# Threshold attention and an ELU feed-forward on one core: another order of the first 45 attention steps, and score rows placed 64 numbers further along the PSUM banks

## The chip, the cores and the metric

The kernel runs on one core of a Trainium2 chip, as one program with one launch. Its engines work side by side, each through its own queue in order: TensorE (PE in the profile, its weight loads PEld), VectorE (DVE), ScalarE (ACT), GpSimd (POOL), and SyncE (SP), which issues nearly all transfers. The metric is the device time of one execution in microseconds (us). Times are given as the median of several executions, and the profile belongs to one execution of its own.

## The reference: what is computed

Eight sequences with eight heads of 576 positions and 64 numbers go through attention in which every score further than `tau` below the maximum of its row is dropped. The result, with the heads side by side, goes through a feed-forward of 512 to 2048 to 512 numbers with ELU between. All is float32; the two weight matrices come as float64, so the kernel has to convert them on the chip.

```python
scores = (q @ k.T) / 8                       # 8 x 8 x 576 x 576
keep   = scores >= max(scores, axis=-1) - tau
attn   = where(keep, exp(scores - max), 0)
attn   = attn / (sum(attn, axis=-1) + 1e-9)
x      = attn @ v                            # -> (8*576, 512)
h      = x @ w_in                            # 512 -> 2048
g      = where(h > 0, h, exp(min(h, 0)) - 1)
out    = g @ w_out                           # 2048 -> 512
```

## The kernel before

**Units of work.** Two heads of a sequence form a pair; there are 32 pairs, four to a sequence. Pair number `pr` has 64 rows of q for one head below 64 for the other, so that the two heads use the two halves of TensorE's rows at once. The queries of a pair are cut into five blocks: blocks 0 to 3 have 128 queries of each head, and block 4 (`NC`) has the remaining 64 queries of both heads as one block of 128 rows. A *step* is one block of one pair: `scores` on TensorE into PSUM, maximum (`max_of`), `exp_of` on ScalarE, `bound_of` on GpSimd, `mask_of` on VectorE (it also sums), sum and reciprocal (`reciprocal_of`), and `normalize` on GpSimd.

The normalized rows are then turned so that keys stand on partitions. There are two ways. `turn_parts` turns them on TensorE, in nine transposes (six for block 4) with an identity matrix, from which ScalarE copies them into the tile `wTa` (blocks 0 and 1, "part 0") or `wTb` (blocks 2 to 4, "part 1"). `turn_squares` transposes squares of 32 by 32 on VectorE, writes the result to DRAM (`there`, four transfers of 144 KB) and `fetch` reads it back in its new order (576 KB). `values` multiplies with v once all blocks of a part are there, and `values_out` copies the result into `xt`, the input of the feed-forward.

**Three stretches.** The first 45 steps (pairs 0 to 8) are written by `early_tasks`. Every operation there is a `task` with a nominal time, a key and the tasks it needs; the value of the key in the table `MOVED` is added to the time, and all tasks are issued in the order of these times, what they need first. So `MOVED` and the nominal times set only the order in which each engine's queue holds its work. A key names the operation, the kind of the step (a letter) and its block. The remaining 23 pairs are written by `tail_step` and `wide_step`, whose scores, two blocks at a time, stand in one PSUM tile of five banks (`wide_scores`); the list `agenda` places the other work there, again with `MOVED`. After the last pair, a stretch of feed-forward alone ends the kernel.

**The first 45 steps in detail.** The order is pair after pair, blocks 0 to 4. The 20 steps of the first sequence have no feed-forward to do, because `xt` of the first sequence is complete only with pair 3. In them `turn_part` puts extra transposes of the identity in front of the real ones (`spare`: 14 in a step, 20 in the earliest, none where the next step's block is 2 or 4); `idle` puts 28 and 16 more at the start. Nothing reads their results. From step 20 on the feed-forward of the first sequence's 512 main rows is done in plain form: `ffn1` (8 units for each of two chunks of 256 rows) and `ffn2_plain` (8 units for each chunk). Each unit is two *halves*, and `SHARES` (steps 20 to 34) and `QUOTA` (steps 35 to 44) say how many halves a step may issue: 14 and 15 in five steps. A half is left for later when the weights it needs are not converted yet (`needs`, `progress`).

The weights come in 32 pieces of 512 KB (`load_w`), and each takes two passes of ScalarE, two of VectorE and one of GpSimd. Seven pieces are handled in steps 4 to 19, then two in a step. Each of the four staging tiles `wst` is loaded again when the piece before in it is finished (`convert_end`), and all these loads go through SP's queue together with those of q, k and v and the squares' transfers.

At step 35 (`SWITCH`) the staging memory is given up for other tiles (`leave_early`). From there all steps turn by squares (`SQUARES`; of the steps before, only step 33 does). In steps 35 to 42 `make_in` forms sums of blocks of w_in on VectorE (three additions each, eight times) and writes them to DRAM, 384 KB each, and in steps 40 to 44 `change_in` changes w_in in place on GpSimd; the later stretches do the feed-forward with seven products instead of eight by them (`first_product`, `second_round`).

Of the kernel before, what the change touches and what calls it, by code (L numbers as in the profile page):

```python
# [18 lines left out]
MOVED = {  # L19
    "adda10": 2.75, "adda40": -0.7, "addb10": -0.45, "addb11": -0.96, "addb20": 0.4, "addb21": 0.54, "addb30": 0.08,  # L20
    "addb31": 0.42, "addb40": -0.13, "addb41": -0.45, "addz40": 1.52, "chd0": -1.67, "chd1": 0.66, "chd3": 5.2,
    "cka3": 1.4, "ckb3": -3.64, "ckc3": -0.46, "ckd3": -1.83, "ckz3": -1.37, "cqa2": 6.78, "cqb2": -3.01,
    "cqc2": -0.22, "cqd2": 2.27, "enda10": 2.38, "enda40": -0.2, "endb00": -0.03, "endb01": 1.48, "endb10": -0.28,
    "endb20": -1.25, "endb21": -1.07, "endb30": 1.25, "endb31": -0.02, "endb40": -0.99, "endb41": 0.29,
    "endz40": 1.58, "exp0a0": 0.24, "exp0a1": -1.03, "exp0a2": 0.05, "exp0a3": 1.07, "exp0a4": -0.35, "exp0b1": -0.97,
    "exp0b2": -0.37, "exp0b3": 1.51, "exp0b4": 0.45, "exp0c0": 0.41, "exp0c1": 3.53, "exp0c2": 0.65, "exp0c4": -0.53,
    "exp0d0": 0.12, "exp0d1": -2.91, "exp0d4": -0.42, "exp0z0": -1.78, "exp0z1": -0.69, "exp0z2": -1.71,
    "exp0z3": 1.1, "exp0z4": -1.32, "exp1a0": 0.27, "exp1a2": -1.45, "exp1b0": -0.12, "exp1b1": -0.6, "exp1b2": 0.26,
    "exp1b3": -0.56, "exp1c0": -1.22, "exp1c1": 1.42, "exp1c3": -0.54, "exp1d1": 0.28, "exp1d3": 0.23, "exp1z0": 4.71,
    "exp1z2": 0.39, "exp1z3": 2.23, "f0.0": -2.08, "f1.0": -0.13, "f1.1": 0.2, "f10.0": 0.05, "f11.0": -0.04,  # L30
    "f12.1": 0.12, "f13.1": -0.5, "f14.0": 0.02, "f15.1": -0.06, "f16.0": 0.04, "f16.1": 0.69, "f16.2": -0.14,
    "f17.0": -0.28, "f18.1": 0.12, "f2.0": -5.54, "f2.1": -0.25, "f2.2": 0.7, "f20.1": -1.03, "f21.0": 0.13,
    "f22.1": -0.19, "f23.0": 0.08, "f23.1": 2.72, "f23.2": 0.07, "f25.0": 0.39, "f26.0": -0.08, "f26.1": 0.42,
    "f3.0": 0.35, "f5.0": -0.32, "f5.1": 4.32, "f6.1": -0.54, "f7.0": -0.01, "f9.0": 0.35, "f9.1": 1.94,
    "fbound0": -0.14, "fbound1": 0.93, "fbound4": -0.36, "fe00": 0.1, "fe10": 0.37, "fe11": 0.3, "fe20": -0.6,
    "fetchc0": 0.68, "fetchc1": 1.8, "fetchc3": 1.11, "fetchc4": 2.68, "fetchd0": -1.89, "fetchd1": -3,
    "fetchd2": 0.42, "fexp00": 0.1, "fexp20": 0.25, "fexp31": 0.12, "ffetch0": 1.19, "ffetch1": -0.24,
    "ffetch2": -0.52, "ffetch3": -0.65, "fkcopy": -0.11, "floadk": -2.59, "floadq": 2.51, "fm00": -3.15,
    "fm01": -0.49, "fm11": -2.07, "fm20": 1.6, "fm21": -0.43, "fmask00": 1.48, "fmask01": -0.63, "fmask10": 0.68,
    "fmask11": 0.02, "fmask30": -0.16, "fmask31": 0.36, "fmask4": 0.2, "fmax00": -0.03, "fmax01": -0.65,  # L40
    "fmax10": 0.91, "fmax11": 0.5, "fmax20": -0.99, "fmax21": -0.15, "fmax30": 0.04, "fmax31": -0.17, "fmax4": 0.36,
# [96 lines left out]
def kernel(  # L138
# [45 lines left out]
    psum = {"t": banks.enter_context(tc.tile_pool(name="ps_t", bufs=2, space=PSUM))}  # L184

    first = ExitStack()
    psum["s"] = first.enter_context(tc.tile_pool(name="ps_s0", bufs=3, space=PSUM))

    ident = wstage.tile([P, P], FP32, name="ident", bufs=1)
    make_identity(nc, ident)  # L190

    tau_sb = const.tile([P, 1], FP32, name="tau_sb")
# [1454 lines left out]
```

## Time and profile before

| | before |
|---|---|
| median of 3 executions | 1311.3 us (1310.9 to 1311.52) |
| the profiled execution | 1310.99 us |
| its span, first to last instruction | 1309.2 us |
| PE busy | 1294.1 us (99%), 6971 instructions |
| PEld busy | 1007.7 us (77%) |
| DVE busy | 1016.5 us (78%) |
| POOL busy | 802.8 us (61%) |
| ACT busy | 559.6 us (43%) |
| DMA | 248.94 MB, mean 190 GB/s |
| first score of steps 10, 20, 35 | 51.57, 96.59, 206.03 us |
| first score of the first `tail_step` | 287.34 us |

Times inside the profile count from the span's start. A group of instructions is named by line, engine and operation, then what it writes and reads by the program's names, its shape, how many there were, busy time and mean duration, and at the end the idle time of the engine before them with what ended it. A float32 matmul is two instructions on TensorE. A table of stretches gives the busy time of each engine in each stretch with its number of instructions in parentheses, the granted TensorE clock (1.00 is full), the mean busy share of the 16 DMA engines and what they moved. A timeline row is start, duration, engine, line, operation, names, form and count of merged neighbours; a matmul's duration includes its way through the array, so its cost in a row of matmuls is read from the distance of the starts.

### The profile page before, as it was taken

The page shows a single profiled execution, that of the slowest core. Times are in us where ns is not written, and L with a number is a line of the kernel's source. Part 1 is how long each engine was busy: PE and PEld are TensorE (multiplying, and loading weights), DVE is VectorE, ACT ScalarE, POOL GpSimd, SP SyncE. Part 2 cuts the span into 40 slices and gives each one's busy share as a digit, 9 for nine tenths or more (in the row PEclk, how much of TensorE's full clock was granted, in tenths as well). Part 3 has the DMA queues.
Part 4 walks back from the last instruction along what each step waited for, and adds up shares of the span by engine and source line. Part 5 has one row for each costly group of instructions (what it writes and reads, how often), then busy time and mean ns, then how long its engine had stood idle before and what let it go on. Part 6 is the DMA issues. An engine that isn't in the chain of part 4 may idle for free.

```text
span 1309.2 us, 21968 instructions
## 1 busy us (share of the span) xinstructions
PE 1294.1 (99%) x6971; PEld 1007.7 (77%) x6971; DVE 1016.5 (78%) x2199; ACT 559.6 (43%) x1216; POOL 802.8 (61%) x1186
## 2 busy tenths in 40 slices
PE   9999999999999999999999999999999999999998
PEld 7667656556788887777777787777777888888887
DVE  6878886879888988898889979897989882545534
ACT  5677763225252535344444434352525260421320
POOL 4667875777466765766576747574858473624533
PEclk9999999999999999999999999999999999999999
DMA  6344655987888988898979888989899875221211
GB/s 138 77 106 125 177 111 140 258 229 219 222 233 237 258 227 251 220 268 209 245 211 264 231 234 225 258 235 240 229 253 256 221 215 173 92 73 60 93 61 33
DMA packets 323379, 248.94 MB, mean 190 GB/s; under 512 B 208832, under 2 KB 285120, under 8 KB 323264
## 3 DMA queue, kind: packets, MB, share of 16 engines
q1 hardware_dynamic: 321328, 247.06, 69.2%
q8 instruction: 55, 0.90, 0.3%
q10 hardware_dynamic: 1936, 0.48, 0.2%
q14 instruction: 60, 0.49, 0.1%
HBM read 162.40 MB, written 85.07 MB: 189 GB/s over the span
## 4 chain that ended last, share of the span: by engine, by line
PE 92%; DVE 4%; DMA 1%; issue 1%; POOL 1%; SPq 1%; ACT 0%; DVEq 0%; POOLq 0%; ACTq 0%
PE f L1378 29%; PE f L1238 29%; PE sc L625 8%; PE sc L685 7%; PE f L776 4%; PE rt L438 3%; PE sc L367 3%; PE f L736 3%; PE pv L578 2%; PE sc L677 1%; PE sc L672 1%; PE pv L573 1%; DVE w L428 1%; DMA there<-x 0%; POOL w L401 0%
## 5 line engine op out<-in xcount | busy, mean ns | idle before, releaser
L401 POOL TENSOR_SCALAR w<-w,rs 128x576 f32<-128x576 f32 x196 | 164.8, 848 | 80.7 <-DVE rs L435 65.5
L632 DVE TENSOR_REDUCE mx<-sc 128x1 f32<-128x576 f32 x207 | 148.2, 749 | 35.7 <-PE sc L625 33.0
L642 ACT ACTIVATE w<-sc,mx 128x576 f32<-128x576 f32 x115 | 83.0, 740 | 114.4 <-DVE mx L632 96.8
L1238 PE MATMUL f<-xt,sw 128*128 128x256 f32 x512 | 123.8, 384 | 0.8 <-ACT xt L695 0.5
L1238 PE MATMUL f<-xt,w_in_sb 128*128 128x256 f32 x512 | 122.4, 381 | 0.3 <-ACT w L1252 0.3
L638 POOL TENSOR_SCALAR th<-mx,ntau 128x2 f32<-128x2 f32 (+1 forms) x115 | 34.3, 298 | 141.2 <-DVE mx L632 141.2
L512 DVE STREAM_TRANSPOSE x<-w 128x512 f32<-128x512 f32 (+2 forms) x146 | 98.1, 706 | 13.5 <-POOL w L401 12.9
L1238 PEld LDWEIGHTS f<-xt,w_in_sb 128*128 128x128 f32 x512 | 96.1, 190 | 16.1 <-ACT w L1252 3.3
L1238 PEld LDWEIGHTS f<-xt,sw 128*128 128x128 f32 x512 | 93.7, 190 | 18.2 <-ACT xt L695 0.9
L625 PE MATMUL sc<-kT,qT 64*128 64x512 f32 (+4 forms) x736 | 107.5, 423 | 0.0
L1238 PE MATMUL f<-x,w_in_sb 128*128 128x256 f32 x448 | 106.1, 379 | 1.3 <-ACT g L1299 1.3
L625 PEld LDWEIGHTS sc<-kT,qT 64*128 64x128 f32 x736 | 80.8, 186 | 34.2 <-issue 16.8
L1378 PE MATMUL f<-w_out_sb,g 128*128 128x256 f32 x448 | 107.1, 382 | 0.0
L1378 PE MATMUL f<-w_out_sb,s 128*128 128x256 f32 x448 | 107.0, 382 | 0.0
L1378 PE MATMUL f<-t,s 128*128 128x256 f32 x448 | 105.8, 379 | 0.0
L1325 POOL TENSOR_TENSOR s<-g 128x256 f32<-128x256 f32 x104 | 80.3, 778 | 29.4 <-PE f L1378 20.1
L646 DVE SCALAR_TENSOR_TENSOR w<-sc,th,w 128x576 f32<-128x576 f32 x115 | 89.7, 810 | 10.3 <-ACT w L642 10.1
L1238 PEld LDWEIGHTS f<-x,w_in_sb 128*128 128x128 f32 x448 | 85.0, 190 | 13.3 <-ACT g L1299 1.7
L1378 PEld LDWEIGHTS f<-w_out_sb,g 128*128 128x128 f32 x448 | 84.1, 190 | 12.9 <-issue 0.7
L1378 PEld LDWEIGHTS f<-t,s 128*128 128x128 f32 x448 | 85.1, 190 | 11.6
L1378 PEld LDWEIGHTS f<-w_out_sb,s 128*128 128x128 f32 x448 | 84.2, 190 | 12.3
L401 POOL TENSOR_SCALAR e<-e,rs 128x576 f32<-128x576 f32 x92 | 68.5, 748 | 35.8 <-DVE rs L435 34.5
(189 smaller groups left out, 2853.7 us busy)
## 6 DMA issues: line engine op xcount, KB each, us to landing
there<-x SPq DMA_DIRECT2D x412, 144.0 KB, 3.5
wTb<-there SPq DMA_DIRECT2D x53, 576.0 KB, 6.3
wTa<-there SPq DMA_DIRECT2D x50, 576.0 KB, 5.0
sw<-win_sums SPq DMA_DIRECT2D x62, 384.0 KB, 4.3
t<-wout_sums SPq DMA_DIRECT2D x45, 512.0 KB, 5.4
qm<-in_q_dram SPq DMA_DIRECT2D x124, 72.0 KB, 4.5
vm<-in_v_dram SPq DMA_DIRECT2D x64, 128.0 KB, 3.4
wst<-in_moe_w_in_dram SPq DMA_DIRECT2D x16, 512.0 KB, 4.0
```

The costliest lines, as they stand in the source:

```text
L367: nc.tensor.matmul(scs[h][:, a, :HALF], qs[r], kT[r, k0 : k0 + HALF], start=True, stop=True)
L401: nc.gpsimd.tensor_scalar(wv, wv, st["rs"][:, h : h + 1], 1.0, ALU.mult, ALU.mult)
L512: nc.vector.transpose(x[:, :, c0 : c0 + nc_], src.rearrange("p (c g n) -> p g c n", c=nc_, n=T))
L625: on_banks(nc.tensor.matmul(o, qT[r, i * P : (i + 1) * P], kT[r, k0 : k0 + n], start=True, stop=True, skip_group_check=True), o)
L632: on_banks(nc.vector.tensor_reduce(st["mx"][:, h : h + 1], st["sc", h], axis=AX.XY if i == NC else AX.X, op=ALU.max, negate=True), st["sc" ...
L642: on_banks(nc.scalar.activation(st["e", h], st["sc", h], AF.Exp, bias=st["mx"][:, h : h + 1]), st["sc", h])
L646: on_banks(nc.vector.scalar_tensor_tensor(st["e", h], st["sc", h], st["th"][:, h : h + 1], st["e", h], ALU.is_ge, ALU.mult, accum_out=st[" ...
L685: on_banks(nc.tensor.matmul(o, vm[:, h, c], parts[part][:, g0:g1, h * (NC + 1) + c], start=False, stop=(c == NC - 1), skip_group_check=Tru ...
L776: nc.tensor.matmul(cur[c, i][:, :DM], hidden(c, ft % NU, 1)[:, 0, ft // NU, i], w_out_sb[:, ft], start=(ft == 0), stop=(ft == NFT - 1))
L1238: nc.tensor.matmul(loc["banks"][place], left[:, j], right[:, j], start=(begins and j == 0), stop=(j == 1), skip_group_check=True)
L1325: engine.tensor_tensor(o, x, y, op)
L1378: nc.tensor.matmul(place(m), lhs, rhs, start=(begins and v == 0), stop=(v == RU - 1), skip_group_check=True)
```

## The change: what it does

**Order.** The first 20 steps become: blocks 0 and 1 of all four pairs (steps 0 to 7), then blocks 2, 3, 4 of all four (steps 8 to 19). So all of part 0 of the first sequence is there after step 7. The constant `LATE = 10` takes the place of `per_seq = 20` wherever the planner distinguishes early from late steps: the PSUM pools change at step 10, and the feed-forward's halves begin there. `SHARES` allows two halves in each of steps 10 to 34, `QUOTA` nine in five steps from 35 on. Extra transposes stand only in steps 0, 1, 3 (20 each) and 5, 7 (14 each); the 28 and 16 at the start remain. A new kind letter `e` names steps 10 to 19.

**What follows from the order.** The q and k of pairs 0 to 3 are prepared one pair in two steps, and must be kept until step 19: pairs 0 and 1 get room in the staging memory, as does their v (two more tiles to be set to zero, `vds_first`). Part 0 of pairs 1 and 3 uses the tile `wTb`. The weights' pieces are handled in steps 3, 5, 7, 9 (one each), then two in a step until step 23. `make_in` is split into its three additions, and six of the eight are placed in steps 26 to 33, in the staging tiles. The sum of a step becomes a task apart from its reciprocal (`total_of`; the instructions are the same). Seven steps before `SWITCH` turn by squares (24, 25, 27, 28, 30, 31, 32) and not 33; from 35 on all do, as before. A second identity is made in the new memory after `leave_early`. The values in `MOVED` for the first 45 steps are new; those of the later stretches (keys that begin with `s` or `f` and a step of these) are the same as before.

**Rows.** In `wide_scores` the four rows of 576 scores start 64 numbers further on in the five banks. [...]

```diff
+    steps[:per_seq] = [(pr, i) for x in ((0, 1), (2, 3, NC)) for pr in range(NPAIR) for i in x]
+    LATE = 10
...
-    QUOTA = ((2, 2), (2, 2), (2, 0), (2, 1), (2, 0))
+    QUOTA = ((1, 1), (1, 1), (1, 1), (1, 0), (1, 1))
-    SQUARES = [*range(SWITCH, MIDDLE), *(n for n in range(per_seq + 2, SWITCH) if MOVED.get(f"sq{n}", 0.0) > 1.0)]
+    SQUARES = [n for n in range(per_seq + 2, MIDDLE) if n >= MIDDLE - 2 or MOVED.get(f"sq{n}", 0.0) * (1 if n < SWITCH else -1) > 1.0 - 2 * (n >= SWITCH)]
...
-        begin = [5.0 * min(n, per_seq) + 7.2 * max(0, n - per_seq) for n in range(MIDDLE + 4)]
+        begin = [5.0 * min(n, LATE) + 7.2 * max(0, n - LATE) for n in range(MIDDLE + 4)]
...
-        slots = [(n, x) for n in range(NB - 1, SWITCH)
-                 for x in range(steps[n][1] in (NB - 1, 1) if n < per_seq else 2)][: len(pieces)]
+        slots = [(n, x) for n in range(3, SWITCH) for x in range(n % 2 if n < LATE else 2)][: len(pieces)]
...
+        for u in range(NU):
+            n = 26 + 3 * u // 2 if u < NU - 2 else SWITCH + u - NU + 2
+            for x in range(3):
+                task(("in", u, x), begin[n] + 4.6 + 1.2 * x, f"in{x}{kind(n)}", lambda u=(u + 2) % NU, x=x: make_in(u, x),
...
-                    if n < per_seq - 1 and x < 2 and not (n > 1 and steps[n + 1][1] in (2, NC)):
-                        spare.append((8 if x else 6) if n >= NB - 1 else (11 if x else 9))
+                    if n < LATE - 1 and x < 2 and not (n >= 2 and n % 2 == 0):
+                        spare.append((8 if x else 6) if n >= 4 else (11 if x else 9))
...
-    SHARES = ((1, 1, 1, 1), (0, 1, 1, 0), (1, 1, 1, 0), (0, 1, 1, 0), (1, 1, 1, 0))
+    SHARES = ((0, 0, 0, 0), (0, 0, 0, 0), (0, 1, 1, 0), (0, 1, 1, 0), (0, 1, 1, 0),
+              (0, 1, 1, 0), (0, 1, 1, 0), (0, 1, 1, 0), (0, 1, 1, 0), (0, 1, 1, 0))
...
-                c = (2 * h + (s ^ h)) * S
+                c = 2 * T + (2 * h + (s ^ h)) * S
                 st["sc", h], st["e", h] = wide[0][:, c : c + S], st["w"][:, h * S : (h + 1) * S]
-        for h, s, c, n in ((0, 0, 0, 512), (1, 1, 0, 384), (0, 0, 512, 64), (1, 1, 384, 192),
-                           (1, 0, 0, 320), (0, 1, 0, 448), (1, 0, 320, 256), (0, 1, 448, 128)):
+        for h, s, c, n in ((0, 0, 0, 448), (1, 1, 0, 320), (1, 1, 320, 256), (0, 0, 448, 128),
+                           (1, 0, 0, 256), (0, 1, 0, 384), (1, 0, 256, 320), (0, 1, 384, 192)):
```

## The prediction

> **What bounds the kernel now.** I read the page's engines and chain first, then a table of stretches over the first 45 steps, then TensorE's groups by shape, then the timeline at two places. The page (first fence) says that TensorE sets the time:
>
> ```profile
> PE 1294.1 (99%) x6971; PEld 1007.7 (77%) x6971; DVE 1016.5 (78%) x2199; ACT 559.6 (43%) x1216; POOL 802.8 (61%) x1186
> ...
> PE 92%; DVE 4%; DMA 1%; issue 1%; POOL 1%; SPq 1%; ACT 0%; DVEq 0%; POOLq 0%; ACTq 0%
> ```
>
> So work taken off TensorE is a gain, if no other engine then becomes the bound. How near the others are is seen in the stretches (columns: stretch, length, busy us of PE, PEld, DVE, ACT, POOL, clock, DMA share, GB/s):
>
> ```profile
> 15.00:55.00 40.00, 39.61 (x290) 29.21 (x290) 30.71 (x76) 28.54 (x62) 23.70 (x45) 1.00 0.53 125
> 55.00:99.00 44.00, 42.66 (x298) 29.15 (x297) 36.20 (x87) 31.01 (x69) 27.05 (x46) 1.00 0.39 91
> ...
> 152.00:185.00 33.00, 32.47 (x146) 16.69 (x143) 29.56 (x59) 24.53 (x49) 28.57 (x34) 1.00 0.67 160
> ...
> 230.00:262.00 32.00, 31.18 (x133) 18.22 (x132) 27.71 (x64) 7.66 (x14) 22.24 (x33) 1.00 0.93 254
> 262.00:287.00 25.00, 24.66 (x93) 11.21 (x91) 20.29 (x44) 5.39 (x11) 18.61 (x30) 1.00 0.85 226
> ```
>
> VectorE is at 77 to 90% and, from 230 us on, the DMA engines at 93%, beside a TensorE at 97% or more. About 90% is the most that VectorE reached beside a full TensorE; I use that as its practical limit.
>
> But not all of TensorE's early time is needed. Its groups over the whole run:
>
> ```profile
> L438 PE MATMUL rt<-ident,w 128*128 128x128 f32 x278 | 46.3, 281 | 3.2 <-POOL w L401 1.5 <-issue 1.0
> L438 PE MATMUL rt<-ident 128*128 128x128 f32 x230 | 31.2, 283 | 1.5 <-POOL ident masks.py:199 1.5
> ...
> L625 PE MATMUL sc<-kT,qT 64*128 64x128 f32 x92 | 17.5, 270 | 0.0
> L625 PE MATMUL sc<-kT,qT 64*128 64x64 f32 x92 | 15.2, 245 | 0.0
> ```
>
> The 230 transposes of the identity alone are the extra ones, which compute nothing. The 92 matmuls of 64 numbers are two in each of the 46 calls of the wide scores.
>
> **The change, part by part.** *Extra transposes.* By the code, before: 20 in steps 0, 1, 2, 14 in nine more steps, 44 at the start: 230, as the row says. After: 3x20 + 2x14 + 44 = 132. One costs 0.109 us, by the starts of merged rows in the timeline:
>
> ```profile
> 30.39 0.82 PE L438 MATMUL rt<-ident 128*128 128x128 f32 x6
> 31.05 0.60 PE L438 MATMUL rt<-ident,w 128*128 128x128 f32 x4
> 31.48 1.04 PE L438 MATMUL rt<-ident 128*128 128x128 f32 x8
> 32.36 0.38 PE L438 MATMUL rt<-ident,w 128*64 128x128 f32 x2
> ```
>
> (18 from 30.39 to 32.36). 98 fewer are 10.7 us of TensorE. What replaces them is real: the 64 halves of feed-forward (1.73 us each from start to start, 110.7 us) are unchanged, but 50 of them now fit into steps 10 to 34 and 14 remain for the last ten steps, where 32 of them run between 204 and 287 us now.
>
> *Real transposes.* 17 steps turn by squares instead of 11. Before, 7 steps x 6 + 27 x 9 = 285 transposes; after, 6 x 6 + 22 x 9 = 234: 51 fewer, 5.6 us. VectorE pays for each of the six steps two transposes of 128x512 (0.686) and one of 128x128 (0.268): 1.64 us, 9.8 in all. Each also issues four writes of 144 KB and a read of 576 KB on SP's queue; spread over steps 24 to 32, where the weights' loads have just ended, I cost them at nothing. Without that cover each delays the queue by its landing, 3.3 us for the write.
>
> *Work moved to other stretches.* VectorE, from its groups: a head's row costs 0.748 (maximum) + 0.809 (mask) + the read of its sum, about 1.57 with overlaps; sum and reciprocal 0.32 a step; a prepared q or k 0.77; a piece of weights 0.62 + 0.77; the ELU of a unit 0.68; a `make_in` 1.76.
> Steps 0 to 9 after: 20 rows 31.4 + 3.2 + preparations 6.3 + four pieces 5.6 = 46.5 us, less overlap 44; TensorE has only 42 of its own. Before it was 18 rows, in 51.57 us with the start-up. So this stretch becomes VectorE's: step 10 starts at 53 (+1.4).
> Steps 10 to 23: TensorE 28 halves 48.4 + scores 15.7 (1.17 a step, 1.0 for block 4) + values 15.3 (3.15 and 2.55 a part) + 114 transposes 13.7 = 93 us; VectorE 24 rows, 28 pieces, 8 units and the rest 85; ScalarE 84 (28 pieces at 1.39, 24 exponentials at 0.74, copies); GpSimd 74. All near their limit: 99 us.
> Steps 24 to 34: TensorE 22 halves 38 + 12.4 + 11.4 + 30 transposes 3.6 = 65.5, VectorE with squares and six `make_in` 60: 68 us.
> Steps 35 to 44: TensorE only 47, VectorE its present 66.5 less six `make_in` (10.6) and eight ELUs (5.2) = 50.5, at 90% 56 us; the DMA engines, busy 65 us from 206 to 287 now, lose six writes of 384 KB and some loads: 51 to 57. So 58 us, no longer TensorE's.
> Sum: 53 + 99 + 68 + 58 = 278 for the first `tail_step`, against 287.34: 9 us earlier. TensorE's work alone would give 16.3; the other 7 go to waits in the first and last ten steps.
>
> *Small parts.* Two more tiles set to zero, 0.21 us each on GpSimd, lie beside TensorE's 28 transposes at the start; the second identity (0.5) beside GpSimd's slack in the last ten steps. The split of sum and reciprocal adds no instruction. Loads of q and k for pairs 2 and 3 move from some 40 us apart to two steps, 9 us, on SP's queue; they land in 2.8 to 3.6 us and DMA's share there is 0.4 to 0.5, so 0, and if a load came late VectorE's transpose and all masks behind it would wait as long. Part 0 in turns in `wTa` and `wTb` gives more time to empty them, not less. `leave_early` now waits for the last early `make_in`'s write too (3.8 us to landing), and step 35's mask waits for it, with VectorE's queue behind; that write belongs to step 33, more than a step of 6 us earlier: 0.
>
> *The rows.* The wide scores take 2.25 us:
>
> ```profile
> 340.25 2.32 PE L625 MATMUL sc<-kT,qT 64*128 64x512 f32 x16
> 342.49 1.99 PE L1378 MATMUL f<-w_out_sb,s 128*128 128x256 f32 x8
> ```
>
> Each half of TensorE's rows streams 1152 columns twice; eight instructions of 256 columns take 1.73 us, so 0.843 ns a column and 1.94 us. About 0.10 goes before the first columns and 0.09 after the last. One half (the one with 384, 192, 320, 256) goes without a break and ends at 342.29. In the other the starts are 340.25, .78, 341.21, .26, .38, .81, 342.18, .29: the 64, 64 and first 448 take 0.60 instead of 0.485, so it ends 0.11 later. After the change the smallest is 128, and two of 128 stand 0.11 apart here, their own length. The halves then end together, 0.11 earlier. After two of 128 the next weights may still come up to 0.05 late. I take 0.09 x 46 = 4.1 us (2.9 to 5.3). These steps are 2.25 us 45 times of 46 with TensorE full, so it is all on the path.
>
> [...] The trace has 1.00 in every stretch, those made mostly of transposes too, and no idle gap of TensorE above 1.4 us after the start. I take 0, and 3 us into the range.
>
> **The sum.** 1310.99 - 9 - 4 = 1298 us for the profiled execution, whose span is 1309.2 with 1.8 around it; the median of the runs lies 0.3 above it, so 1298 serves for both. 0.2% of 1311.3, 2.6 us, is about what a measurement can tell from no change.
>
> **Rivals.**
> *TensorE stays the bound throughout* (0.15). Then 16.3 + 4.1 come off: 1290.6. For it: 97% or more in every stretch now, and an order of the queues in which idle stretches are filled by later halves. Against it: in the last ten steps 47 us of TensorE stand against 50 of VectorE.
> *The others eat the early gain; only the rows remain* (0.14): 1307. For it: VectorE at 90% in 152 to 185, with fewer pieces a microsecond than steps 10 to 23 will need. Against it: it needs some 9 us more of waits than I have.
> *The weights become the bound, and the kernel slower* (0.11). Pieces 7 to 31 take from 98 to 187 us now, 3.7 us each; I need 3.5 (28 in 99 us), and the first chunk's units come due just when their pieces end, two pieces to a unit. A tile is loaded, converted by five passes in three queues and only then loaded again, behind a wait in SP's queue, where the loads of q, k and v and squares stand too; ScalarE, VectorE and GpSimd hold exponentials and masks behind a late piece. The price is 28 us for each microsecond per piece. At 3.83 my gain from the order is gone; from 4.1 on (16 us more) it outweighs the rows as well and the total is over 1314. For it: VectorE waited for a piece's landing 3.1 us in one place. Against it: tiles were reloaded up to two pieces ahead and TensorE never waited long for them.
> [...]
>
> **How the numbers follow.** Likeliest 0.55, 1298, its own range 1293 to 1303 (some 5 us of error in four stretches, 1 in the rows). The three rivals 0.15, 0.14, 0.11, and 0.05 for what lies between the second and third, within 2.6 us of before. Faster 0.84, same 0.05, slower 0.11. The range from 1289 (TensorE's bound, with the rows at their best) to 1309 leaves out the last two cases.
>
> **What would show it.** The identity alone x132 and the transposes of `w` x234; no 64x64 form in the wide scores and 2.16 us from their start to the next matmul (2.25: rows wrong); step 10 near 53, step 24 near 152, step 35 near 220, the first `tail_step` near 278 us; in the last ten steps a TensorE below 90%, released by VectorE or by the squares' transfers. The forecast is wrong if the pieces end later than about 156 us, if the clock falls below 1.00, or if the later stretch, whose order is untouched, no longer repeats every 68.55 us less 0.36.

## The result, and the profile after

| | before | after |
|---|---|---|
| median, beside each other on one chip | 1311.52 us (1310.9 to 1312.93) | 1306.12 us (1305.41 to 1307.49) |
| ratio | | 0.9958 [0.9947, 0.9969] |
| profiled execution, its span | 1310.99, 1309.2 us | 1305.87, 1304.1 us |

The change makes the kernel 5.4 us faster. The forecast was 13.3 us. The time is inside the forecast's whole range (1289 to 1309 us), but outside that of its likeliest case (1293 to 1303). It lies where the second rival put it (1307 us): the early gain is eaten, and the rows remain.

The page after, engines, the clock's row and the chain:

```profile
PE 1278.2 (98%) x6822; PEld 994.8 (76%) x6822; DVE 1022.4 (78%) x2218; ACT 552.0 (42%) x1196; POOL 800.6 (61%) x1190
...
PEclk9999999899999999999999999999999999999999
...
PE 85%; DVE 5%; POOL 3%; issue 2%; DMA 1%; ACT 1%; SPq 1%; DVEq 0%; POOLq 0%; ACTq 0%
```

TensorE is busy 15.9 us less, but the span is only 5.1 us shorter. TensorE's share of the chain falls from 92 to 85%, GpSimd's rises from 1 to 3%, and one slice of the clock's row is an 8.

The work went as planned. TensorE's groups by shape have the 132 transposes of the identity and 228 + 6 of `w`:

```profile
L471 PE MATMUL rt<-ident,w 128*128 128x128 f32 x228 | 36.1, 279 | 5.3 <-POOL w L427 4.8 <-ACT wTb L488 0.4
L471 PE MATMUL rt<-ident 128*128 128x128 f32 x132 | 19.2, 302 | 1.5 <-POOL ident masks.py:199 1.5
...
L471 PE MATMUL rt<-ident,w 128*64 128x128 f32 x6 | 1.6, 272 | 0.0
```

The table of stretches, from the first score to step 10, to step 24, to step 35 and to the first `tail_step` (stretch, length, busy us of PE, PEld, DVE, ACT, POOL, clock, DMA share, GB/s), shows where the time went:

```profile
7.29:56.05 48.76, 46.55 (x338) 33.58 (x337) 41.99 (x95) 33.34 (x65) 28.14 (x50) 1.00 0.68 148
56.05:152.98 96.93, 93.36 (x479) 61.22 (x478) 79.86 (x167) 74.34 (x153) 77.14 (x98) 1.00 0.51 153
152.98:221.79 68.81, 67.76 (x338) 45.75 (x336) 58.10 (x134) 26.81 (x54) 31.57 (x57) 1.00 0.67 180
221.79:284.72 62.93, 54.80 (x206) 25.58 (x205) 49.28 (x113) 16.81 (x33) 48.21 (x73) 0.95 0.80 219
sum 277.43, PE 262.48 PEld 166.14 DVE 229.23 ACT 151.30 POOL 185.06; mean PE 65.62 PEld 41.53 DVE 57.31 ACT 37.82 POOL 46.27
```

The last ten steps of the kernel before, and its sum from the first score on:

```profile
206.03:287.34 81.31, 79.09 (x335) 47.58 (x335) 66.51 (x143) 21.31 (x41) 57.37 (x82) 1.00 0.81 221
sum 281.23, PE 275.66 PEld 180.21 DVE 226.56 ACT 158.58 POOL 189.77; mean PE 68.92 PEld 45.05 DVE 56.64 ACT 39.65 POOL 47.44
```

Between its first score and the first tail step, TensorE now idles 277.43 - 262.48 = 14.95 us; before, the same sum gave 281.23 - 275.66 = 5.57. More than half of the idle time after, 8.1 us, is in the last ten steps, where the clock is at 0.95.

The timeline there (start, duration, engine, line, operation, names; idle time and its releaser at the end):

```profile
242.08 1.24 PE L393 MATMUL sc<-kT,qT 64*128 64x288 f32 x8
...
243.71 0.74 POOL L427 TENSOR_SCALAR w<-w,rs 128x576 f32<-128x576 f32 x1
244.44 0.27 POOL L435 TENSOR_SCALAR th<-mx,ntau 128x1 f32<-128x1 f32 x1
244.65 0.52 POOL L346 COPY qd<-qT 64x64 f32<-64x64 f32 x2
...
245.26 0.75 POOL L427 TENSOR_SCALAR w<-w,rs 128x576 f32<-128x576 f32 x1
...
246.04 1.50 DVE L550 STREAM_TRANSPOSE x<-w 128x512 f32<-128x512 f32 x3 [1.23 <-POOL w L427]
...
247.67 0.82 DVE L454 SCALAR_TENSOR_TENSOR w<-sc,th,e 128x576 f32<-128x576 f32 x1
...
248.65 1.30 PE L393 MATMUL sc<-kT,qd 128*128 128x288 f32 x2 [5.33 <-DVE w L454]
```

This is step 39, the first block 4 among the last ten steps. Its scores wait 5.33 us for step 38's mask (L454 on VectorE). The mask waits in VectorE's queue behind the square transposes of step 37's rows (L550). These wait for step 37's second normalization (L427 on GpSimd), which stands behind a bound and the copies into `qd`. A step's rows lie in the tile `w`, of which the late memory holds one: step 38's mask can't write it before step 37's rows are turned. So from step 35 on each step is a loop from mask to sum, reciprocal, normalization, squares and the next mask. The kernel before has the same loop, but 13 halves of feed-forward lay over it between the scores of step 35 and those of step 39 (33.27 us apart); now there are 7 (26.86 us apart).

Inside this idle time, at 245.82 us, the clock falls to half for 6.83 us; the scores of step 39 take 2.26 us instead of 1.13.

At the other end of the change, the wide scores (the first line is one of 46, the others the first of all):

```profile
339.11 2.21 PE L663 MATMUL sc<-kT,qT 64*128 64x448 f32 x16
341.25 0.70 PE L1441 MATMUL f<-w_out_sb,s 128*128 128x256 f32 x2
...
289.49 1.02 PE L663 MATMUL sc<-kT,qT 64*128 64x448 f32 x4
291.92 1.67 PE L663 MATMUL sc<-kT,qT 64*128 64x256 f32 x12 [1.42 <-DVE w L684]
293.52 0.70 PE L1301 MATMUL f<-xt,w_in_sb 128*128 128x256 f32 x2
```

From start to the next matmul 2.14 us, 2.24 before; the median of the 46 fell from 2.248 to 2.141. The third takes 3.06 us in both kernels. The first one of all takes 4.03, and in it TensorE waits 1.42 us for VectorE's mask. Before, it took 2.25.

### The profile page after: what moved, and what is told of

The parts are those of the page before. It is cut to its first block, busy times and chain, and to the rows that moved or that the text cites. A ratio compares the mean times of both kernels' runs of the same rounds, so it can differ in the third digit from the quotient of the medians.

```text
span 1304.1 us, 21747 instructions
## 1 busy us (share of the span) xinstructions
PE 1278.2 (98%) x6822; PEld 994.8 (76%) x6822; DVE 1022.4 (78%) x2218; ACT 552.0 (42%) x1196; POOL 800.6 (61%) x1190
## 4 chain that ended last, share of the span: by engine, by line
PE 85%; DVE 5%; POOL 3%; issue 2%; DMA 1%; ACT 1%; SPq 1%; DVEq 0%; POOLq 0%; ACTq 0%
PE f L1441 30%; PE f L1301 28%; PE sc L663 7%; PE sc L723 7%; PE f L774 3%; PE sc L393 3%; PE rt L471 2%; PE f L814 2%; PE pv L616 1%; POOL w L427 1%; DVE w L454 1%; PE sc L715 1%; PE sc L710 1%; DVE mx L431 1%; DMA there<-x 1%
## 5 line engine op out<-in xcount | busy, mean ns | idle before, releaser
L427 POOL TENSOR_SCALAR w<-w,rs 128x576 f32<-128x576 f32 x196 | 163.1, 841 | 88.5 <-DVE rs L468 85.7
L550 DVE STREAM_TRANSPOSE x<-w 128x512 f32<-128x512 f32 (+2 forms) x163 | 107.2, 692 | 13.9 <-POOL w L427 13.6
L1301 PEld LDWEIGHTS f<-xt,w_in_sb 128*128 128x128 f32 x512 | 96.2, 190 | 15.9 <-ACT w L1315 2.7
L663 PE MATMUL sc<-kT,qT 64*128 64x448 f32 (+4 forms) x736 | 103.2, 416 | 1.4 <-DVE w L684 1.4
L1301 PEld LDWEIGHTS f<-x,w_in_sb 128*128 128x128 f32 x448 | 85.0, 190 | 13.3 <-ACT g L1362 1.8
L427 POOL TENSOR_SCALAR e<-e,rs 128x576 f32<-128x576 f32 x92 | 68.5, 748 | 35.3 <-DVE rs L468 33.8
```

The costliest lines, as they stand in the source:

```text
L427: nc.gpsimd.tensor_scalar(wv, wv, st["rs"][:, h : h + 1], 1.0, ALU.mult, ALU.mult)
L550: nc.vector.transpose(x[:, :, c0 : c0 + nc_], src.rearrange("p (c g n) -> p g c n", c=nc_, n=T))
L663: on_banks(nc.tensor.matmul(o, qT[r, i * P : (i + 1) * P], kT[r, k0 : k0 + n], start=True, stop=True, skip_group_check=True), o)
L1301: nc.tensor.matmul(loc["banks"][place], left[:, j], right[:, j], start=(begins and j == 0), stop=(j == 1), skip_group_check=True)
```

## The experiments

Two theories stood against each other at first. *Theory:* the rows bring 46 x 0.107 = 4.9 us, and the order brings nothing, because what it takes off TensorE was filling; the pace of the early steps is set by VectorE and GpSimd in the order of their queues. *Rival:* TensorE's work is the bound, and the order loses its gain at single places (the gap at step 39, the first wide scores) that can be repaired by moving work into them.

"Behind the first score" counts from a profile's own first score, because that one lies anywhere from 6.1 to 7.6 us, whatever the kernel. Each ratio is to the kernel before as measured beside that run, whose medians were 1311.20 to 1311.62 us. The edits of the changed kernel were not measured beside it, so differences from it of less than about 1 us are not read. The last two columns are single profiles, in us:

| run | median us | ratio to before [interval] | first score to first tail step | from there to the end |
|---|---|---|---|---|
| before | 1311.52 | | 281.23 | 1021.86 |
| after | 1306.12 | 0.9958 [0.9947, 0.9969] | 277.42 | 1019.37 |
| rows_alone | 1307.04 | 0.9966 [0.9955, 0.9978] | 280.99 | 1016.92 |
| order_alone | 1310.86 | 1.0002 [0.9993, 1.0010] | 277.61 | 1023.73 |
| rows_swap | 1306.74 | 0.9963 [0.9951, 0.9976] | 277.58 | 1019.09 |
| cover38 | 1309.63 | 0.9987 [0.9978, 0.9996] | 276.37 | 1022.59 |
| norms_first | 1305.88 | 0.9957 [0.9944, 0.9969] | 276.87 | 1019.21 |
| pe_turn2 | 1307.49 | 0.9969 [0.9958, 0.9980] | 281.23 | 1018.60 |
| hold3 | 1311.21 | 0.9997 [0.9988, 1.0006] | 283.94 | 1019.60 |
| hold6 | 1310.7 | 0.9995 [0.9986, 1.0004] | 283.54 | 1017.16 |
| gp_in | 1306.77 | 0.9968 [0.9956, 0.9980] | 279.50 | 1018.65 |
| gp_in_hold6 | 1309.56 | 0.9991 [0.9982, 0.9999] | 285.10 | 1017.25 |
| nofill_before | 1317.51 | 1.0046 [1.0033, 1.0058] | 287.26 | 1021.84 |
| nofill_after | 1306.95 | 0.9970 [0.9960, 0.9981] | 280.24 | 1019.37 |
| fewfill_before | 1310.62 | 0.9993 [0.9984, 1.0002] | 279.37 | 1021.86 |
| clock_kept | 1303.79 | 0.9940 [0.9927, 0.9952] | 275.22 | 1019.58 |
| clock_norms | 1302.19 | 0.9929 [0.9916, 0.9943] | 274.74 | 1018.85 |

### Each part alone

The kernel before with the new rows (rows_alone), and the changed kernel with the old rows (order_alone):

```diff
-                c = (2 * h + (s ^ h)) * S
+                c = 2 * T + (2 * h + (s ^ h)) * S
...
-        for h, s, c, n in ((0, 0, 0, 512), (1, 1, 0, 384), (0, 0, 512, 64), (1, 1, 384, 192),
-                           (1, 0, 0, 320), (0, 1, 0, 448), (1, 0, 320, 256), (0, 1, 448, 128)):
+        for h, s, c, n in ((0, 0, 0, 448), (1, 1, 0, 320), (1, 1, 320, 256), (0, 0, 448, 128),
+                           (1, 0, 0, 256), (0, 1, 0, 384), (1, 0, 256, 320), (0, 1, 384, 192)):
```

> The old order of the first 45 steps, with the rows of the wide scores moved by 64 numbers. Theory (the rows pay in each of the 46 wide scores, 2.25 to 2.14 us): 46 x 0.107 = 4.9 us less than before, near 1306.6, so nearly the whole gain of the changed kernel. Rival (the rows pay less, because the first wide scores wait 1.4 us for a mask wherever the rows are moved): 3 us less, 1308.5, with a wait of TensorE for VectorE's mask inside the first wide scores.

> The new order, with the rows of the wide scores where they were. Theory (the order brings the first tail step 2.6 us forward and nothing after it changes): near 1308.9, 2 to 3 us less than before; the wide scores at 2.25 us, the first of them without a wait. Rival (the first wide scores wait because of the new order): the first wide scores take about 3.7 us here too, and the total is about 1310.

The rows alone are faster by 0.34%. The order alone can't be told from the kernel before. In the profiles, the time from the first tail step to the end falls by 1021.86 - 1016.92 = 4.94 us with the rows alone; 45 of the 46 calls are shorter by 0.107 us each, 4.8 in all, and the medians are 4.2 us apart. The order alone saves 281.23 - 277.61 = 3.6 us up to the first tail step and gives 1.9 of them back behind it; its first wide scores take 3.92 us, with 1.14 of waiting for VectorE. The same gap and halved clock stand at its step 39:

```profile
249.01 2.26 PE L393 MATMUL sc<-kT,qd 128*128 128x288 f32 x4 [5.31 <-DVE w L454]
```

### The first wide scores: which matmul waits

The change also exchanges two of the eight matmuls. Exchanged back:

```diff
-        for h, s, c, n in ((0, 0, 0, 448), (1, 1, 0, 320), (1, 1, 320, 256), (0, 0, 448, 128),
+        for h, s, c, n in ((0, 0, 0, 448), (1, 1, 0, 320), (0, 0, 448, 128), (1, 1, 320, 256),
```

> The changed kernel with the third and fourth matmul of the wide scores exchanged back: the rest of row 0 (bank 1) before the rest of row 2 (bank 3). Theory (the first wide scores wait 1.4 us because bank 3, which holds the tail's scores until their mask, is now asked for as the third instead of the fourth): the wait in the first wide scores falls below 0.7 us, the other 45 stay at 2.14, total 1 to 1.5 us less than the changed kernel. Rival (the mask comes late, and any order waits for it): no difference within 0.4 us.

The first wide scores take 4.03 us again, with a wait of 1.20: the mask before is late, and this order of the eight waits for it too. The median of the 46 is 2.142 us: it is the new lengths that pay (the four rows as 448+128, 320+256, 256+320, 384+192 columns instead of 512+64, 384+192, 320+256, 448+128), not the order of these two.

### Filling the gap at step 39, shortening it, or avoiding what makes it

One more half of feed-forward may be issued in steps 38 and 43 (cover38):

```diff
-    QUOTA = ((1, 1), (1, 1), (1, 1), (1, 0), (1, 1))
+    QUOTA = ((1, 1), (1, 1), (1, 1), (1, 1), (1, 1))
```

> The changed kernel with one more half of feed-forward (1.73 us) allowed in steps 38 and 43, behind their scores. Theory (step 39's scores wait 5.3 us because TensorE has no feed-forward left to lay between step 38's scores and theirs, and the wait halves the clock): the gap of TensorE before step 39's scores falls to 3.6 us or less, the clock there stays at or near 1.00, the first tail step comes 2 to 4 us earlier. Rival (VectorE, GpSimd and the transfers bound the last ten steps together): the gap moves to a later step and the first tail step comes within 1 us of 284.7.

The gap at step 39 falls to 3.40 us and the clock stays full there. But the last ten steps still have 15 halves in all, steps 39 to 44 have one less, and the wait stands at the first tail step (timeline of this run):

```profile
276.15 1.21 PE L393 MATMUL sc<-kT,qd 128*128 128x288 f32 x4 [0.90 <-DVE w L454]
282.45 1.22 PE L710 MATMUL sc<-kT,qT 64*64 64x288 f32 x4 [5.09 <-DVE w L454]
283.60 1.22 PE L611 MATMUL pv<-wTa,vd 128*128 128x256 f32 x2
284.75 3.39 PE L616 MATMUL pv<-wTa,vm 128*64 128x256 f32 x16
```

The 16 matmuls of L616 take 3.39 us at half clock, 1.95 at full. The median is 3.5 us above the changed kernel's. The profile belongs to the shortest execution (1306.83 us), so it shows where the wait went, but not all of these 3.5 us.

The two normalizations of step 37 (block 2, letter `c`) earlier in GpSimd's queue (norms_first):

```diff
-"norm0c2": 2.56
+"norm0c2": -0.6
-"norm1c2": -0.12
+"norm1c2": -0.6
```

> The changed kernel with both normalizations of step 37 placed on GpSimd's queue ahead of the scaling of the next pair's q. Theory (the gap before step 39's scores is one chain: normalize, square transposes, mask; GpSimd did other work for 2 us in it): the gap falls from 5.3 to about 3.3 us, the clock may stay at 1.00, but the end of the stretch does not follow in full: total 0 to 3 us below the changed kernel. Rival (the gap alone is the loss, 7 us with the clock): total 4 to 6 us below it.

The gap falls to 4.00 us, the clock is halved for 3.41 us instead of 6.83, and the first tail step comes 0.55 us earlier behind the first score. So the normalizations are in the chain that makes the gap, as read above. The gain in the median, 0.24 us, can't be measured.

Steps 37 and 38 turned on TensorE instead of by squares (pe_turn2):

```diff
-"sq37": -4.13, "sq38": -0.32
+"sq37": 2, "sq38": 2
```

> The changed kernel with steps 37 and 38 turned on TensorE (nine transposes each) instead of by squares on VectorE and through DRAM. Theory (VectorE's chain through the squares bounds the last ten steps while TensorE idles): 3.3 us less on VectorE, 2 us more on a TensorE that waits; the 5.3 us gap before step 39's scores shrinks by 1.5 us or more and the first tail step comes 1.5 to 4 us earlier. Rival (transfers or the order of the queues bound it): the first tail step within 1 us of 284.7, or later, because the transposes stand in front of scores in TensorE's queue.

VectorE's squares are out of the loop of these steps, but the normalization is not (timeline):

```profile
242.78 0.89 PE L393 MATMUL sc<-kT,qT 64*128 64x288 f32 x6
246.41 1.80 PE L471 MATMUL rt<-s,w 128*128 128x128 f32 x9 [2.74 <-POOL w L427]
249.21 1.32 PE L393 MATMUL sc<-kT,qd 128*128 128x288 f32 x2 [0.99 <-DVE w L454]
```

TensorE now waits for GpSimd, the clock halves all the same, and the first tail step is 3.8 us later than after the change.

### Are steps 24 to 34 TensorE's, VectorE's, or a chain's?

Steps 20, 25 and 30 (hold3), and also 23, 28 and 33 (hold6), issue one half instead of two; the halves go to the last ten steps:

```diff
-              (0, 1, 1, 0), (0, 1, 1, 0), (0, 1, 1, 0), (0, 1, 1, 0), (0, 1, 1, 0))
+              (0, 1, 0, 0), (0, 1, 1, 0), (0, 1, 1, 0), (0, 1, 0, 0), (0, 1, 1, 0))
...
-    QUOTA = ((1, 1), (1, 1), (1, 1), (1, 0), (1, 1))
+    QUOTA = ((1, 1), (1, 1), (1, 1), (1, 1), (1, 1))
```

> The changed kernel with one half of feed-forward instead of two in steps 20, 25 and 30, so that three halves (5.2 us of TensorE) move from the stretch of steps 20 to 34 into steps 35 to 44. Theory (up to step 34 TensorE is the bound, from step 35 on VectorE's chain of mask, normalize, square transposes and next mask is, and TensorE has idle time there): step 35 starts 4 to 5 us earlier, steps 35 to 44 take no longer than now (62.9 us), total 3 to 5 us below the changed kernel. Rival (VectorE bounds both stretches, at 86 to 95%): step 35 starts less than 2 us earlier and the total is within 1.5 us of the changed kernel.

> The same with six halves held back (steps 20, 25, 30 and 23, 28, 33) and two halves allowed in every step from 35 on, 10.4 us of TensorE moved. Theory (TensorE idle from step 35 on): step 35 starts 7 to 10 us earlier, steps 35 to 44 take 62 to 65 us without a gap above 3 us, total 6 to 9 us below the changed kernel. Rival (VectorE bounds both stretches): total within 2 us of the changed kernel, gaps of TensorE behind GpSimd's normalize in steps 23 to 34.

The additions of `make_in` on GpSimd instead of VectorE (gp_in), and this with the six halves held (gp_in_hold6):

```diff
-        nc.vector.tensor_tensor(sw[:, x], a, b, ALU.add)
+        nc.gpsimd.tensor_tensor(sw[:, x], a, b, ALU.add)
```

> The changed kernel with the 24 additions of make_in on GpSimd instead of VectorE: 18 of them, 8.7 us of VectorE, lie in steps 24 to 34, where GpSimd is busy less than half of the time. Theory (VectorE with its queue order sets the pace of steps 24 to 34): these steps take 2 to 6 us less than 68.8 us, and step 35 starts that much earlier after the first score; the total is 1 to 5 us less than the changed kernel's. Rival A (TensorE sets it there, with its halves): steps 24 to 34 stay within 1 us of 68.8 us and TensorE stays as busy as it was. Rival B (GpSimd's normalizations, queued behind the slower additions, come late): steps 24 to 34 take longer, with VectorE and TensorE waiting for GpSimd.

> As the run before, with six halves of feed-forward (10.4 us of TensorE) taken out of steps 20 to 33 and issued in the last ten steps. Theory (with VectorE relieved as well, both engines have room in steps 24 to 34, and the last ten steps fill their gaps): step 35 starts 5 to 9 us earlier behind the first score than in the changed kernel (214.5 us), the largest gap of TensorE in the last ten steps stays under 3.5 us, so the clock stays full there, and the total is 3 to 6 us under the changed kernel's. Rival (a chain of dependent steps through GpSimd sets both stretches, whichever engine is relieved): step 35 at most 3 us earlier, the total within 2.5 us of the changed kernel's or above it.

Steps 24 to 34 of hold6, gp_in and gp_in_hold6, in this order, as rows of their tables of stretches:

```profile
152.44:218.96 66.52, 63.63 (x306) 40.43 (x304) 56.28 (x132) 25.23 (x52) 29.93 (x55) 1.00 0.67 182
```

```profile
152.69:221.45 68.76, 68.09 (x338) 45.96 (x336) 50.74 (x116) 26.68 (x54) 41.20 (x75) 1.00 0.68 184
```

```profile
153.28:218.83 65.55, 62.84 (x306) 40.58 (x304) 49.30 (x114) 25.44 (x52) 39.97 (x73) 1.00 0.69 187
```

7.4 us off VectorE alone: nothing (68.76 against 68.81), TensorE is busy 99%. So my theory of VectorE's work as this stretch's bound fell, and rival A of gp_in stands. Two halves off TensorE (hold3, 2 x 1.73 = 3.5 us in this stretch): 68.69 us, nothing either. Four halves (6.9 us) bring 2.3 us, and these with 8.8 us off VectorE 3.3. TensorE is full, and close behind it stands something that neither engine's load moves much. Dependent steps in the order of the queues are my reading of it; no run here separates them. What is held back then costs more in the last ten steps. All four runs are slower than the changed kernel or equal to it, so work can't be shifted there with profit: TensorE waits 3.23 us and 2.19 us in hold6's last ten steps, 3.23 and 3.11 in gp_in_hold6's. In hold3 and hold6, 17 and 20 halves instead of 15 didn't close the gap before step 39's scores (5.31 and 3.23 us). In gp_in_hold6 no gap of the last ten steps reached the 3.5 us up to which I had expected a full clock (cover38 kept it with 3.40, norms_first lost it with 4.00): 3.23 us was the longest. The clock still halved, at 250.74 us for 3.41 us.

### What the extra transposes were worth

The kernel before without the 186 extra transposes inside its first 20 steps (nofill_before), with 78 of them left out (fewfill_before), and the changed kernel without its 88 (nofill_after):

```diff
-                    if n < per_seq - 1 and x < 2 and not (n > 1 and steps[n + 1][1] in (2, NC)):
-                        spare.append((8 if x else 6) if n >= NB - 1 else (11 if x else 9))
```

```diff
-                        spare.append((8 if x else 6) if n >= NB - 1 else (11 if x else 9))
+                        spare.append((5 if x else 3) if n >= NB - 1 else (7 if x else 5))
```

```diff
-                    if n < LATE - 1 and x < 2 and not (n >= 2 and n % 2 == 0):
-                        spare.append((8 if x else 6) if n >= 4 else (11 if x else 9))
```

> The kernel before without the 186 extra transposes of the identity inside its first 20 steps (the 44 at the start stay); they compute nothing, so all results are computed as before. Theory (TensorE's busy share in the first steps is filling; VectorE, ScalarE and GpSimd in the order of their queues set the pace there): step 20 starts no more than 3 us earlier than before's 96.59 and the total is within 3 us of before, unless single gaps of TensorE reach some 4 us, where the granted clock should halve and cost 1 to 3 us. Rival (the extra transposes are on the path that sets the end, as my sum took them to be): 186 x 0.109 = 20 us earlier at step 20 and in the total.

> The kernel before with 78 of the 186 extra transposes of the identity left out of its first 20 steps (12 instead of 20 in the earliest steps, 8 instead of 14 in the others); all results are computed as before. Theory (they only fill what VectorE, ScalarE and GpSimd leave, and keep the clock): step 20 starts 90.5 us behind the first score as before, within 1.5 us, and the total is within 2 us of before, as long as the granted clock stays 1.00. Rival (they are on the path, as my sum had it): 78 x 0.109 = 8.5 us earlier at step 20 and in the total.

> The changed kernel without the 88 extra transposes of the identity in its first steps (the 44 at the start stay). Theory (others set the pace there): step 10 starts no more than 2 us earlier than in the changed kernel's profile (56.05, 48.8 us behind the first score), the total within 2.5 us of it. Rival (they are on the path): 88 x 0.109 = 9.6 us earlier at step 10 and in the total. A third outcome, slower by over 2 us, would say that they keep the clock: the granted clock of the first 50 us would then show halved stretches.

fewfill_before, from its first score to step 20:

```profile
6.92:96.55 89.63, 83.06 (x557) 55.14 (x556) 71.28 (x172) 61.48 (x132) 51.54 (x96) 1.00 0.47 109
```

Before, this took 90.48 us with TensorE busy 89.17. 8.5 us of transposes less bring 0.85 us there by these two profiles, and 1.0 in the median, which can't be told from none. They were filling; about a tenth of them at most was on the path.

Without all of them the kernel gets slower by 6 us, which neither my theory nor its rival had as the size: step 20 comes 7.0 us later behind the first score. The clock is the reason that the table of stretches shows (nofill_before):

```profile
12.30:15.70 3.40, 1.99 (x10) 1.13 (x10) 2.71 (x6) 2.74 (x6) 2.57 (x5) 1.00 0.83 139
15.70:22.60 6.90, 6.57 (x24) 4.47 (x24) 4.43 (x13) 3.79 (x9) 2.92 (x9) 0.51 0.84 258
36.20:39.60 3.40, 1.89 (x10) 1.09 (x10) 3.33 (x10) 2.55 (x8) 1.74 (x3) 1.00 0.47 154
39.60:43.00 3.40, 3.22 (x13) 2.12 (x13) 2.40 (x7) 2.30 (x5) 2.30 (x4) 0.51 0.00 0
49.90:53.30 3.40, 2.33 (x14) 1.71 (x15) 3.06 (x9) 2.57 (x5) 1.60 (x4) 1.00 1.00 254
```

A stretch of 3.4 us in which TensorE is busy 1.99 or 1.89 us (55 to 58%) is followed by half a clock, one with 2.33 us (69%) is not. The longest single gap of TensorE in these steps is 1.45 us, far below the 4.00 us of norms_first. 20.5 us of the first 91 run at half clock. In nofill_after's profile it is 13.7 us of the first 37, and step 10 comes 2.7 us later. That profile is of an execution of 1308.3 us with a mean clock of 0.992; four of the seven have 0.995 and take 1306.21 to 1306.95, and the median is 0.8 us over the changed kernel's, too near to be called a difference. So the transposes' use is the clock. 108 of them were enough for it in fewfill_before, 88 in the profiles of the changed kernel and ten of its eleven edits that keep them (hold3 is the exception).

### The halved clock in the last ten steps

36 transposes of the second identity (26 in clock_norms) between the scores of steps 38 and 39; clock_norms has the edit of norms_first too:

```diff
+        def hold_clock(n):
+            room_for("t", lambda: None)
+            rt = psum["t"].tile([P, NC, P], FP32, name="rt", tag="rt")
+            for _ in range(n):
+                transpose(rt[:, 0], idents[-1])
...
+            if n == SWITCH + 3:
+                task("clock", t + 5.0, None, lambda: hold_clock(36))
```

> The changed kernel with 36 transposes of the second identity (3.9 us) between the scores of step 38 and those of step 39, where TensorE idles 5.33 us and the clock then falls to half; nothing else is moved. Theory (the clock costs some 2 us of the last ten steps by itself): the granted clock stays 1.00 there, the scores of step 39 start at the same time but take 1.13 us instead of 2.26, the first tail step comes 1.5 to 2.5 us earlier behind the first score (275 to 276 us instead of 277.4), and the total falls by about as much, to some 1304. Rival (VectorE's and GpSimd's chain sets the end whatever the clock is): the scores of step 39 are quicker, but TensorE waits longer later; the first tail step and the total stay within 0.7 us.

> As the run before (26 transposes), with the two normalizations of norms_first issued earlier, which shortens the gap at step 39 from 5.33 to 4.0 us. Theory: the two gains add, the first tail step comes 2.5 to 3.5 us earlier behind the first score than in the changed kernel (274 to 275 us), the total is 1302 to 1304.5, below both kernels. Rival (the chain takes it back before or in the first wide step): the first tail step within 1 us of norms_first's 276.9, the total 1305 or more.

clock_kept, timeline at step 39 and the last ten steps' row of the table of stretches:

```profile
241.76 1.24 PE L393 MATMUL sc<-kT,qT 64*128 64x288 f32 x8
242.93 4.15 PE L471 MATMUL rt<-s 128*128 128x128 f32 x36
248.32 0.97 PE L393 MATMUL sc<-kT,qd 128*128 128x288 f32 x3 [1.24 <-DVE w L454]
```

```profile
221.49:282.42 60.93, 56.90 (x242) 28.42 (x241) 49.18 (x113) 16.79 (x33) 48.10 (x73) 1.00 0.83 226
```

The scores of step 39 start as late as before (26.83 us behind step 35, 26.86 in the changed kernel): the chain is untouched. The clock is 1.00, the stretch takes 60.93 us instead of 62.93, and the median falls by 2.3 us to 1303.79. Work that computes nothing makes the kernel faster.

clock_norms takes 59.61 us for the stretch and 1302.19 us in all, 9.3 us less than before and 3.9 less than after, ahead of both kernels. Its first tail step is 2.1 us earlier behind the first score than norms_first's. The medians of these two lie 3.7 apart, more than that; norms_first's profile was of its shortest execution (1304.11 us). The mean clocks of norms_first's five executions are 0.996 to 0.998, those of clock_norms 0.999 to 1.000.

A second tile `w` in the late memory (4.5 KB a partition), which would cut the loop directly, wasn't tried.

## Why the prediction was wrong, step by step

The sum was 53 + 99 + 68 + 58 = 278 us for the first tail step, then 4 us for the rows. Term by term, the profile of after has 56.05 + 96.93 + 68.81 + 62.93 = 284.72, 6.7 us more. With 1.9 us lost at the first wide scores, which the sum didn't have, and 0.8 gained over the 4.1 of the rows, 1298 becomes 1305.8; 1305.87 was measured. The steps that failed are the waits of the last ten steps, the clock put at 0, and the handover to the wide steps left out. That steps 10 to 23 took 2.1 us less than their term was luck: it hid a part of this.

- **"So 58 us, no longer TensorE's" for steps 35 to 44: 62.93, the largest miss.** I took VectorE's 50.5 us of work at 90%. Its work was right (49.28 us busy). What I had not looked for is the loop through the one tile `w` with GpSimd in it: VectorE is at 78%, and waits for the normalization. The sign that I gave came true, with TensorE at 87% and released by VectorE; the size of the waits did not. TensorE was busy 54.80 us and not 47, with 15 halves instead of 14 and 6.83 us at half clock among them. 2.0 of the 4.9 us are the clock behind the gap (clock_kept), 1.3 the place of step 37's normalizations (clock_norms against clock_kept), and 1.6 are not divided further.
- **"I take 0, and 3 us into the range" for the clock.** The clock fell below 1.00, which I had named as a sign of being wrong. No run shows the 3 us; keeping the clock at 1.00 in the last ten steps was worth 2.0 us there and 2.3 in the median (clock_kept). A gap of 5.33 us came with half clock for 6.83 us, one of 4.00 (norms_first) for 3.41, and one of 3.40 (cover38) with none. But the length of the gap doesn't decide it alone: waits of 2.19 and 3.23 us in hold6 were followed by 3.41 us each. I took 0 because the trace of before had 1.00 in every stretch and no such gap, although my own forecast had TensorE waiting in just these ten steps. That was the wrong way to read a trace: one without such waits doesn't show what they cost. Transposes were enough to keep it: 36 of them hold the clock at 1.00 in clock_kept, and in the profiles of before and after the clock became full (at 4.47 and 6.89 us) while TensorE had done nothing but the 28 transposes at the start.
- **"step 10 starts at 53 (+1.4)": 56.05.** 1.2 us are the later first score (7.29 against 6.11), which changes from execution to execution. The other 1.9 are less clear. I had called this stretch VectorE's, with 44 us of work against 42 of TensorE; of its 48.76 us, VectorE is busy 41.99 (86%) and TensorE 46.55, idle 2.2. Which of the two sets its length is not shown.
- **Steps 10 to 23, "99 us", and 24 to 34, "68 us".** 96.93 and 68.81. The weights' pieces were no bound; the rival that made the kernel slower didn't come. TensorE's own work, 93 and 65.5 us by my count, is 93.36 and 67.76. In steps 10 to 23 the others were not near their limit as I had said: TensorE is busy 96%, VectorE 82, GpSimd 80 and ScalarE 77.
- **"98 fewer are 10.7 us of TensorE".** Counted rightly, worth little: by fewfill_before about a tenth of such transposes at most is on the path. TensorE's busy time up to the first tail step fell by 13.2 us, or some 15 without the halved clock's share. Its idle time rose by 9.4, and the clock took 2: that leaves the 3.8 us by which the first tail step is nearer to the first score. My "other 7 go to waits" was the right item, too small by 2.4 and without the clock.
- **The handover to the wide steps** was missing from the sum. TensorE reached them earlier, VectorE didn't, and the first wide scores waited 1.42 us. In hold6, where the first tail step comes 6 us later, they take 2.14 without a wait. With this the order's 3.8 us fall to some 2, and order_alone shows no gain that can be measured.
- **The rows**: right in what they change and nearly in size, 0.107 us a call instead of 0.09. The number of weight loads is the same (736), and 45 of the 46 calls are shorter by 0.107 us. By my estimate, with 0.843 ns a column added to their last starts, the two halves of TensorE's rows end 0.10 us apart before and within 0.01 us now, as forecast.

## What to carry to other kernels

An engine at 98% may be full of work that only fills: leave a part of it out on the chip before its time is counted as a gain. Where a change makes the bounding engine wait, look for the loop that will be next (here one tile, written, read and written again by two other engines), not only for the next engine's load, and price the clock: a forecast with waits of several microseconds can't take the clock from a profile that has none (here a wait of 5.33 us came with half clock for 6.83 us). A gap that can't be closed can be filled; 26 useless transposes and two normalizations moved were worth more here than the new order of 45 steps.

## What the runs showed of the hardware that was not expected

- The halved stretches in these profiles were 3.41 us (norms_first), 6.83 (the changed kernel) or 10.24 us long (nofill_after), except at the end. In the changed kernel the one at step 39 begins 245.82 - 6.89 = 238.93 us, 70 times 3.413, behind the moment when the clock became full; in the kernel before, the one at the end begins 1308.36 - 4.47 = 1303.89 us behind it, 382 times 3.413. There was not one long gap before each of them (1.45 us at most in nofill_before), and the busy share alone doesn't tell them apart either. Two stretches with the same work of TensorE, from nofill_before and from the kernel before:

```profile
12.33:15.74 3.41, 1.99 (x10) 1.13 (x10) 2.72 (x6) 2.78 (x6) 2.59 (x5) 1.00 0.83 140
```

```profile
311.67:315.08 3.41, 1.99 (x8) 1.44 (x8) 3.38 (x11) 2.43 (x5) 2.81 (x7) 1.00 0.99 272
```

Half clock follows the first, full clock the second. Stretches with 41% (gp_in_hold6) and 47% (cover38) kept the full clock, too. What decides stays open.
- The same early work can fall on either side of it. In hold3, the clock halved at 38.14 us for 3.41 us, in steps that this edit doesn't touch, and step 10 came 2.2 us later behind the first score than in the changed kernel's profile. Executions of one kernel differ in it as well: in gp_in_hold6 the seven with a mean clock of 0.998 or 0.999 took 1308.23 to 1310.50 us, the four with 0.996 or 0.997 took 1310.85 to 1312.98.
- The first score lies between 6.08 and 7.55 us. In the kernel before it starts at 6.11 us and the clock became full at 4.47; in the changed kernel it starts at 7.29 and the clock became full at 6.89, with the same 28 transposes that start at 1.46 us in both. That is a spread of 1.5 us between single profiles, to be taken off before stretches are compared.
